# Making T4 of a two-level Strassen unit by an accumulating DMA on the GpSimd queue

## The chip, the cores and the metric

The kernel runs on one core of a Trainium2 chip. The metric is device time in microseconds (us), from the start of an execution to its end. TensorE (PE in the profile) multiplies matrices into PSUM; VectorE (DVE) and ScalarE (ACT) work on tensors in PSUM and SBUF; GpSimd (POOL) and SyncE (SP) are used here mainly to issue DMAs. Each engine works through its own queue in order and waits on semaphores for the others. A DMA that SP or GpSimd issues is carried out by 16 DMA engines that all queues share.

## The reference

The input x0 is 16384 x 1024 in bf16, there are six weight matrices ws of 1024 x 1024 and six biases bs. Each of the six layers computes

```python
x = x0
for l in range(L):                       # L = 6
    proj = jnp.einsum('bd,de->be', x, ws[l]) + bs[l]
    x = x0 * proj + x
```

## The kernel before

The rows of x0 are taken in 16 pairs of 1024 rows. A *unit* is one pair in one layer, so there are 96 units, u = 0 to 95. Inside a unit the activations lie transposed in SBUF (features on the partitions), in four quadrants B11, B12, B21, B22 of 512 features by 512 rows. `blk(xs, dh, n)` is such a quadrant, 128 partitions x 2048 bf16; B21 is `blk(xs, 1, 0)`. For the first layer of a pair they are read from the tile `x0T`, for the later ones from `xst`. There are two of each, used by alternate pairs.

The 1024 x 1024 product is done by the Strassen-Winograd scheme with seven half-size products P1 to P7 in place of eight. On the side of the activations it needs four combinations, each one VectorE instruction over 128 x 2048 (line 202):

- T1 = B12 - B11, T2 = B22 - T1, T3 = B22 - B12, T4 = B21 - T2 (lines 369 to 372).

On the side of the weights it needs the matrices W5, W6, W7, W3. They are formed once per layer, during pair 0, by `combo` (line 312), and kept in HBM in `Lc` (stored by the GpSimd queue, line 306). From pair 1 on they are loaded again for every unit, like the raw quadrants, by SP through `pump` (line 250) into a ring of 16 tiles `wp` of 512 KB. A steady unit uses nine such tiles.

The products chain in PSUM. There are four banks `pA0..3` and four banks `pX0..3`, one for each block m of 128 output features; a `group` (line 289) is four matmuls of 128 x 512 for one m. For each m:

- P1.m goes to pA[m]; P6.m, W6 times T2, is added onto it;
- F.m (ScalarE, line 294) copies pA[m] to pX[m]; P3.m, W3 times B22, is added there, and E3.m (line 298) evacuates it with the bias;
- P7.m, W7 times T3, is added onto pA[m], and E7.m evacuates it;
- P4.m, W4 times T4, is added onto pA[m], and E4.m evacuates it.

In the *steady* units, 6 to 94 (89 of them), products P5 and P2 are done by a second Strassen level, in 2 x 7 smaller groups (line 411), on quarter-size combinations of T1 and of B21 in the `ti` tiles. The units of pair 0 and the last unit (seven in all, `one` is true) do P5 and P2 in one level. After the evacuations VectorE multiplies by x0, adds x and so writes the quadrants of the next layer's x. At the end of a pair the result is turned by DMA transposes (line 538) and stored (line 544), and the x0 of a later pair is loaded by DMA transposes.

The order of the work is written out. Every operation has a rank; for steady units the table `R2` (line 26, and `EARLY[6]`, `EARLY[7]` for the first two) gives it within a unit, and a unit takes 23.4 units of rank. A heap at the end of the kernel (lines 600 to 612) issues the operation with the lowest rank among those whose predecessors have been issued. Predecessors follow from the lists of names that each operation reads and writes. The order found so is the order of every engine's queue; each engine then waits where its data is not there yet. In R2, P6 has the ranks 8.26, 9.13, 12.16 and 13.03, P3 10.86 and 13.89 to 15.62, P7 16.48 to 19.07 and P4 19.93 to 22.52. T2 has 6.93 and T4 8.4. Between the last group of P6 and the first of P4 there are three groups of P3 and the four of P7, 28 matmuls.

No operation of a steady unit uses the GpSimd queue; it stores the weight combinations of pair 0 (the last of them until about 162 us) and a part of the last unit's output.

Of the kernel before, what the change touches and what calls it, by code (L numbers as in the profile page):

```python
# [9 lines left out]
ADD = mybir.AluOpType.add  # L10
SUB = mybir.AluOpType.subtract
# [137 lines left out]
def kernel(  # L149
# [7 lines left out]
    nc = tc.nc  # L157
# [4 lines left out]
    KH = KD // 2  # L162
# [18 lines left out]
    pA = [psum.tile([P, NB], FP32, name=f"pA{i}") for i in range(KH)]  # L181
    pX = [psum.tile([P, NB], FP32, name=f"pX{i}") for i in range(KH)]
    x0Ts = [work.tile([P, 2, KD, NB], BF16, name=f"x0T{i}") for i in range(2)]
    xsts = [work.tile([P, 2, KD, NB], BF16, name=f"xst{i}") for i in range(2)]
    T = {i: work.tile([P, KH, NB], BF16, name=f"T{i}") for i in (1, 2, 3, 4)}
# [12 lines left out]
    def blk(t, dh, n):  # L198
        return t[:, n, dh * KH:(dh + 1) * KH, :]

    def tt(o, a, b, op):
        nc.vector.tensor_tensor(out=o, in0=a, in1=b, op=op)  # L202
# [50 lines left out]
    def ring_make(u, w):  # L253
        pump()
        assert ring_seq[pos["next"]] == (u, w, "make"), (u, w, ring_seq[pos["next"]])
        t = ring_tile(u, w)
        assert t is not None
        pos["next"] += 1
        return t
# [4 lines left out]
    def op(rank, fn, rd=(), wr=(), weights=()):  # L264
        for k in weights:
            uses_left[k] = uses_left.get(k, 0) + 1
        ops.append((rank, fn, tuple(rd), tuple(wr), tuple(weights)))
# [3 lines left out]
    for u, (pr, l) in enumerate(units):  # L271
        one, first, last = level1(u), u == 0, u == NU - 1
# [5 lines left out]
        XI = X0 if l == 0 else XO  # L278

        def add(name, fn, rd=(), wr=(), weights=(), rk=rk, base=base, u=u):  # L280
            op(base + rk[name], fn, rd, wr, [(u, w) for w in weights])

        def ttop(name, o, a, b, o_, rd, wr, **kw):
            add(name, lambda: tt(o, a, b, o_), rd, wr, **kw)

        def group(name, w, bank, bname, rhs, rname, m, start, u=u):
            def fn():
                for k in range(KH):
                    nc.tensor.matmul(bank[:], lhsT=wt[(u, w)][:, k, m * P:(m + 1) * P], rhs=rhs[:, k, :],  # L289
                                     start=(start and k == 0), stop=(k == KH - 1), skip_group_check=True)  # L290
            add(name, fn, rname + [f"w{u}.{w}" + ("a" if name in ("P5.0", "P5.1") and u == 0 else "")] if pr == 0 else rname, [bname], [w])

        def copy(name, dst, src, rd, wr):
            add(name, lambda: nc.scalar.copy(out=dst, in_=src), rd, wr)  # L294

        def biased(name, dst, src, eh, m, rd, wr, l=l):
            c = l * KD + eh * KH + m
            add(name, lambda: nc.scalar.activation(out=dst, in_=src, func=IDENT, bias=b_all[:, c:c + 1], scale=1.0), rd, wr)  # L298

        late = []  # L300
        if pr == 0:
            raw = lambda w, u=u: wt[(u, w)]

            def save(w, t, rd, weights=(), l=l):
                def fn():
                    nc.gpsimd.dma_start(Lc[l, CIDX[w]].rearrange("p (k e) -> p k e", k=KH), t()[:])
                if first:
                    late.append(lambda add=add: add("s" + w, fn, rd + ["gate"], (), weights))
                else:
                    add("s" + w, fn, rd, (), weights)  # L310

            def combo(w, a, b, o_, deps, u=u, raw=raw):
                def part(sl):
                    tt(raw(w)[:, :, sl], raw(a)[:, :, sl], raw(b)[:, :, sl], o_)

                def fn():
                    ring_make(u, w)
                    part(slice(0, HQ) if w == "5" and u == 0 else slice(0, H))
                rd = [f"w{u}.{d}" for d in deps]
                if w == "5" and first:  # L320
                    add("c5", fn, ["ringmake"], ["w0.5a", "ringmake"], [a, b])
                    add("c5b", lambda part=part: part(slice(HQ, H)), ["w0.5a"], ["w0.5"], [a, b])
                else:
                    add("c" + w, fn, rd + ["ringmake"], [f"w{u}.{w}", "ringmake"], [a, b])
                save(w, lambda raw=raw, w=w: raw(w), [f"w{u}.{w}"], [w])

            if first:
                gate = const.tile([P, 1], BF16, name="gate")
                late.append(lambda add=add, xst=xst, XO=XO: add("gate", lambda: nc.gpsimd.tensor_copy(gate[:], xst[:, 0, 0, 0:1]), [XO[0, 0]], ["gate"]))
            combo("5", "w12", "4", ADD, ())  # L330
            combo("6", "5", "1", SUB, ("5",))
            combo("7", "1", "w12", SUB, ())
            combo("3", "2", "6", SUB, ("6",))
            for X, s in (("2i", isum[2 * (l % 2)]), ("5i", isum[2 * (l % 2) + 1])):
                a = lambda r, c, X=X, u=u: wt[(u, X[0])][:, r * KQ:(r + 1) * KQ, c * HQ:(c + 1) * HQ]
                sv = s[:].rearrange("p q (k e) -> p q k e", k=KQ)
                rn = lambda i, X=X, l=l: f"{X}{l % 2}.{i}"
                src = [f"w{u}.5"] if X == "5i" else []

                def icombo(i, fn, rd):  # L340
                    add(X + i, fn, [rn(r) for r in rd] + src, [rn(i)], [X[0]])
                icombo("5", lambda a=a, sv=sv: tt(sv[:, 0], a(0, 1), a(1, 1), ADD), ())
                icombo("6", lambda a=a, sv=sv: tt(sv[:, 1], sv[:, 0], a(0, 0), SUB), "5")
                icombo("3", lambda a=a, sv=sv: tt(sv[:, 2], a(1, 0), sv[:, 1], SUB), "6")
                icombo("7", lambda a=a, sv=sv: tt(sv[:, 3], a(0, 0), a(0, 1), SUB), ())
                save(X, lambda s=s: s, [rn(i) for i in "5637"])

        B11, B12, B21, B22 = blk(xs, 0, 0), blk(xs, 0, 1), blk(xs, 1, 0), blk(xs, 1, 1)
        A = [f"A{m}" for m in range(KH)]
        Xn = [f"X{m}" for m in range(KH)]  # L350
        if first:

            for i, (d, n) in enumerate(TURNED):
                for k in range(KH):
                    xb = k if i < 2 else 2 + k % 2
# [11 lines left out]
                nc.vector.tensor_copy(out=b_all[:], in_=pA[KH - 1][:, 0:LK])  # L367
            add("bT", turn_bias, [], [A[KH - 1]])
        ttop("T1", T[1][:], B12, B11, SUB, [XI[0, 1], XI[0, 0]], ["T1"])
        ttop("T2", T[2][:], B22, T[1][:], SUB, [XI[1, 1], "T1"], ["T2"])  # L370
        ttop("T3", T[3][:], B22, B12, SUB, [XI[1, 1], XI[0, 1]], ["T3"])
        ttop("T4", T[4][:], B21, T[2][:], SUB, [XI[1, 0], "T2"], ["T4"])
        if not one:
            for X, Bm, src in (("5", T[1][:], "T1"), ("2", B21, XI[1, 0])):
                q = lambda dh, n, Bm=Bm: Bm[:, dh * KQ:(dh + 1) * KQ, n * NQ:(n + 1) * NQ]
# [15 lines left out]
        if not one:  # L391
            for X, Bm, src, a, b, C in (("5", T[1][:], "T1", 0, 1, P5s), ("2", B21, XI[1, 0], 2, 3, Q)):
# [5 lines left out]
                def inner(i, bank, start, X=X, u=u, q=q, t_=t_):  # L398
# [4 lines left out]
                    def fn():  # L403
# [27 lines left out]
                     ip5[X][:].unsqueeze(1).to_broadcast([P, 2, KQ, NQ]), ADD, [X + "u0", X + "u1", X + "ps"],  # L431
                     cn(0, 1) + cn(1, 1))
        for m in range(KH):
            xb = m
            group(f"P6.{m}", "6", pA[m], A[m], T[2], ["T2", A[m]], m, False)
            copy(f"F.{m}", pX[xb][:], pA[m][:], [A[m]], [Xn[xb]])
            group(f"P3.{m}", "3", pX[xb], Xn[xb], B22, [XI[1, 1], Xn[xb]], m, False)
            biased(f"E3.{m}", U[:, m, :], pX[xb][:], 0, m, [Xn[xb]], [f"U.{m}"])
            group(f"P7.{m}", "7", pA[m], A[m], T[3], ["T3", A[m]], m, False)
            biased(f"E7.{m}", V[:, m, :], pA[m][:], 1, m, [A[m]], [f"V.{m}"])  # L440
            group(f"P4.{m}", "4", pA[m], A[m], T[4], ["T4", A[m]], m, False)
            if not (last and m == KH - 1):
                biased(f"E4.{m}", W[:, m, :], pA[m][:], 1, m, [A[m]], [f"W.{m}"])
        allm = lambda s: [f"{s}.{m}" for m in range(KH)]
# [200 lines left out]
```

## Time and profile before

| | us |
|---|---|
| median of 3 runs | 2270.74 (2270.19 to 2270.76) |
| profiled execution, span | 2269.4 |
| TensorE busy | 2248.5 (99%) |
| VectorE busy | 2092.1 (92%) |
| ScalarE busy | 1847.8 (81%) |
| one 128 x 2048 subtraction on VectorE | 1.219 |
| a 512 KB weight load, issue to landing, median | 4.7 (from Lc), 5.2 (from ws) |
| a 512 KB store by the GpSimd queue, median | 6.1 (wp), 6.8 (isum) |

The profile is that of one execution, taken by the hardware profiler; its span lies 1.3 us under the median of the runs. *Busy* is the time in which an engine carries out instructions; PEld is TensorE's loading of weights, which overlaps its matmuls. The *chain* follows the work that ended last back to the start: at every step to what released it. In a row of the timeline or of a group, `out<-in` gives the tiles written and read, and xN the number of instructions. The DMA share is the mean busy share of the 16 DMA engines; since records of packets overlap it can be somewhat over 1. Times in windows are counted from the start of the span.

### The profile page before, as it was taken

What the parts mean: (1) busy time and instruction counts of PE and PEld (TensorE: products, weight loads), DVE (VectorE), ACT (ScalarE), POOL (GpSimd) and SP (SyncE); (2) the same over time, 40 slices, a digit from 0 to 9 for tenths busy, and PEclk for the clock granted to TensorE, in tenths of its full rate; (3) what the DMA queues carried; (4) which work ended last, traced back from release to release, by engine and by line L of the source; (5) the groups of instructions that cost most, each with busy time, mean ns of one, the idle gap of its engine ahead of it and who ended that gap; (6) DMA issues with size and microseconds to landing.
All of it is one profiled execution on the core that took longest, in us unless ns stands there. A gap on an engine that the chain in (4) does not pass through costs nothing.

```text
span 2269.4 us, 34750 instructions
## 1 busy us (share of the span) xinstructions
PE 2248.5 (99%) x12754; PEld 1267.4 (56%) x12993; DVE 2092.1 (92%) x2331; ACT 1847.8 (81%) x3234; POOL 24.5 (1%) x46
## 2 busy tenths in 40 slices
PE   9999999999999999999999999999999999999998
PEld 4455555555555555555555555555555555555554
DVE  8999999999999999999999999999999999999997
ACT  6678888888888888888888888888888888888887
POOL 1110000000000000000000000000000000000000
PEclk9999999999999999999999999999999999999999
DMA  8779797796977969779697796977969689696872
GB/s 279 229 270 301 251 249 264 220 303 206 251 259 224 288 220 248 264 218 288 215 266 251 227 285 205 277 242 227 288 201 294 225 225 294 195 295 224 236 247 66
DMA packets 620492, 557.02 MB, mean 245 GB/s; under 512 B 391456, under 2 KB 546592, under 8 KB 620320
## 3 DMA queue, kind: packets, MB, share of 16 engines
q1 hardware_dynamic: 614240, 534.58, 78.6%
q0 software_dynamic: 5488, 19.93, 2.3%
q8 instruction: 102, 1.67, 0.3%
q14 instruction: 70, 0.57, 0.1%
q10 hardware_dynamic: 592, 0.27, 0.0%
HBM read 437.79 MB, written 52.43 MB: 216 GB/s over the span
## 4 chain that ended last, share of the span: by engine, by line
PE 99%; issue 1%; DMA 0%; ACT 0%; SPq 0%; DVE 0%; ACTq 0%
PE pA L289 58%; PE pX L411 24%; PE pX L289 17%; DMA ev<-in_x_dram 0%; ACT pX L294 0%; PE pA L505 0%; PE pX L359 0%; PE pX L505 0%; DVE x0T L516 0%; ACT ev L294 0%; ACT x0T L363 0%; ACT ip L294 0%; SPq L577 0%; SPq L574 0%; ACTq L294 0%
## 5 line engine op out<-in xcount | busy, mean ns | idle before, releaser
L289 PEld LDWEIGHTS <-wp 128*128 128x128 bf16 x7904 | 772.9, 98 | 838.1 <-issue 0.9
L289 PE MATMUL pA<-T,wp 128*128 128x512 bf16 x4468 | 1033.0, 379 | 7.3
L298 ACT ACTIVATE ev<-pA,b_all 128x512 bf16<-128x512 f32 x1123 | 717.5, 692 | 211.2 <-PE pA L289 164.0
L411 PEld LDWEIGHTS <-wp 128*128 128x128 bf16 x4984 | 487.7, 98 | 151.5 <-issue 0.2
L202 DVE TENSOR_TENSOR ev<-ev,x0T 128x2048 bf16<-128x2048 bf16 (+2 forms) x483 | 483.0, 1002 | 8.1 <-ACT ev L298 1.5
L202 DVE TENSOR_TENSOR ev<-ev,ev 128x2048 bf16<-128x2048 bf16 (+1 forms) x283 | 343.9, 1216 | 71.7 <-ACT ev L298 44.6
L202 DVE TENSOR_TENSOR xst<-ev,xst 128x2048 bf16<-128x2048 bf16 x319 | 389.1, 1220 | 19.1 <-PE pX L289 0.9
L411 PE MATMUL pX<-ti,wp 128*128 128x256 bf16 x2848 | 397.8, 273 | 0.0
L298 ACT ACTIVATE ev<-pX,b_all 128x512 bf16<-128x512 f32 x412 | 285.4, 697 | 63.8 <-PE pX L289 62.9
L289 PE MATMUL pX<-xst,wp 128*128 128x512 bf16 x1371 | 323.3, 379 | 0.3
L289 PE MATMUL pA<-xst,wp 128*128 128x512 bf16 x1205 | 302.4, 379 | 3.9
L294 ACT CAST ev<-pX 128x512 bf16<-128x512 f32 x384 | 232.1, 606 | 47.9 <-ACT ev L298 37.4
L294 ACT COPY pX<-pA 128x512 f32<-128x512 f32 x412 | 237.5, 602 | 21.7 <-PE pA L289 18.7
L294 ACT COPY pX<-pX 128x512 f32<-128x512 f32 x356 | 207.8, 584 | 8.6 <-ACT ip L294 0.2
L202 DVE TENSOR_TENSOR T<-xst 128x2048 bf16<-128x2048 bf16 x160 | 195.0, 1218 | 0.3
L202 DVE TENSOR_TENSOR T<-xst,T 128x2048 bf16<-128x2048 bf16 x160 | 195.0, 1219 | 0.2
L294 ACT CAST iu<-pX 128x512 bf16<-128x512 f32 x356 | 192.7, 601 | 0.0
L202 DVE TENSOR_TENSOR ev<-iu,ip 128x1024 bf16<-128x1024 bf16 x178 | 123.2, 692 | 60.7 <-ACT iu L294 60.7
L411 PE MATMUL pX<-T,wp 128*128 128x256 bf16 x1068 | 160.2, 273 | 0.0
L294 ACT CAST ip<-pX 128x512 bf16<-128x512 f32 x178 | 104.7, 589 | 54.0 <-PE pX L411 54.0
L411 PE MATMUL pX<-xst,wp 128*128 128x256 bf16 x888 | 133.2, 273 | 0.1
L202 DVE TENSOR_TENSOR xst<-ev,x0T 128x2048 bf16<-128x2048 bf16 x64 | 78.3, 1223 | 1.6
(50 smaller groups left out, 636.4 us busy)
## 6 DMA issues: line engine op xcount, KB each, us to landing
wp<-Lc SPq DMA_DIRECT2D x538, 512.0 KB, 4.7
wp<-in_ws_dram SPq DMA_DIRECT2D x287, 512.0 KB, 5.2
out_dram<-x0T SPq DMA_DIRECT2D x30, 1024.0 KB, 8.8
Lc<-wp POOLq DMA_DIRECT2D x24, 512.0 KB, 6.1
Lc<-isum POOLq DMA_DIRECT2D x12, 512.0 KB, 6.8
w<-in_ws_dram SPq DMA_DIRECT2D x5, 512.0 KB, 6.1
ev<-in_x_dram SPq DMA_DIRECT2D x3, 512.0 KB, 7.2
out_dram<-x0T SPq DMA_DIRECT2D x3, 256.0 KB, 4.2
```

The lines of the kernel that those rows point to most:

```text
L202: nc.vector.tensor_tensor(out=o, in0=a, in1=b, op=op)
L289: nc.tensor.matmul(bank[:], lhsT=wt[(u, w)][:, k, m * P:(m + 1) * P], rhs=rhs[:, k, :], start=(start and k == 0), stop=(k == KH - 1), skip ...
L294: add(name, lambda: nc.scalar.copy(out=dst, in_=src), rd, wr)
L298: add(name, lambda: nc.scalar.activation(out=dst, in_=src, func=IDENT, bias=b_all[:, c:c + 1], scale=1.0), rd, wr)
L411: nc.tensor.matmul(pX[bank][:, m * NQ:(m + 1) * NQ], lhsT=wv[:, k, m * P:(m + 1) * P], rhs=rhs[:, k, :], start=(start and m == 0 and k == ...
```

## The change

In the steady units T4 is no longer a VectorE instruction with a tile of its own. T2 is formed with the other sign, T1 - B22. A DMA on the GpSimd queue then adds B21 onto T2 in place, element by element, so that the tile holds B21 + T1 - B22 = T4, and P4 reads that tile. Since P6 reads the same tile with its earlier content, the DMA comes after all four groups of P6; to that end the loop that adds P6 and F is split from the one that adds P3, P7 and P4. W6 is formed with the other sign, so that P6 stays the same, and W3's formula, which contains W6, is turned to match. T4's rank stays the same, but its name now reads and writes "T2". The seven units with one level make T4 on VectorE as before, with the sign turned.

```diff
-            combo("6", "5", "1", SUB, ("5",))
+            combo("6", "1", "5", SUB, ("5",))
             combo("7", "1", "w12", SUB, ())
-            combo("3", "2", "6", SUB, ("6",))
+            combo("3", "2", "6", ADD, ("6",))
...
-        ttop("T2", T[2][:], B22, T[1][:], SUB, [XI[1, 1], "T1"], ["T2"])
+        ttop("T2", T[2][:], T[1][:], B22, SUB, [XI[1, 1], "T1"], ["T2"])
         ttop("T3", T[3][:], B22, B12, SUB, [XI[1, 1], XI[0, 1]], ["T3"])
-        ttop("T4", T[4][:], B21, T[2][:], SUB, [XI[1, 0], "T2"], ["T4"])
+        if one:
+            ttop("T4", T[4][:], B21, T[2][:], ADD, [XI[1, 0], "T2"], ["T4"])
+        else:
+            pass
+        T4 = (T[4], "T4") if one else (T[2], "T2")
...
         for m in range(KH):
+            group(f"P6.{m}", "6", pA[m], A[m], T[2], ["T2", A[m]], m, False)
+            copy(f"F.{m}", pX[m][:], pA[m][:], [A[m]], [Xn[m]])
+        if not one:
+            add("T4", lambda B21=B21: nc.gpsimd.dma_start(T[2][:], B21, accum_op=ADD), [XI[1, 0], "T2"], ["T2"])
+        for m in range(KH):
             xb = m
-            group(f"P6.{m}", "6", pA[m], A[m], T[2], ["T2", A[m]], m, False)
-            copy(f"F.{m}", pX[xb][:], pA[m][:], [A[m]], [Xn[xb]])
             group(f"P3.{m}", "3", pX[xb], Xn[xb], B22, [XI[1, 1], Xn[xb]], m, False)
             biased(f"E3.{m}", U[:, m, :], pX[xb][:], 0, m, [Xn[xb]], [f"U.{m}"])
             group(f"P7.{m}", "7", pA[m], A[m], T[3], ["T3", A[m]], m, False)
             biased(f"E7.{m}", V[:, m, :], pA[m][:], 1, m, [A[m]], [f"V.{m}"])
-            group(f"P4.{m}", "4", pA[m], A[m], T[4], ["T4", A[m]], m, False)
+            group(f"P4.{m}", "4", pA[m], A[m], T4[0], [T4[1], A[m]], m, False)
```

## The prediction

> **What bounds the kernel now.** I read the page's busy times first, then the chain that ended last, the groups that touch the T tiles, the timeline around one steady unit's P6 to P4, and last how busy the DMA engines are in that stretch. From the page (busy time, two DMA queues, the chain by engine, two groups):
>
> ```profile
> PE 2248.5 (99%) x12754; PEld 1267.4 (56%) x12993; DVE 2092.1 (92%) x2331; ACT 1847.8 (81%) x3234; POOL 24.5 (1%) x46
> q1 hardware_dynamic: 614240, 534.58, 78.6%
> q0 software_dynamic: 5488, 19.93, 2.3%
> PE 99%; issue 1%; DMA 0%; ACT 0%; SPq 0%; DVE 0%; ACTq 0%
> L289 PE MATMUL pA<-T,wp 128*128 128x512 bf16 x4468 | 1033.0, 379 | 7.3
> L202 DVE TENSOR_TENSOR T<-xst,T 128x2048 bf16<-128x2048 bf16 x160 | 195.0, 1219 | 0.2
> ```
>
> TensorE is the chain: 99% of it, and 2269.4 - 2248.5 = 20.9 us of idle time in the whole span. Matmuls that read a T tile were preceded by 7.3 us of idle time in all. So whatever VectorE gains can give back next to nothing, and a new wait of TensorE is paid in full. The page also prices the GpSimd queue's DMA: q0 moved 38 x 512 KB, and its packets took 2.3% of sixteen engines for 2269.4 us, so 52.2 / 38 = 1.37 us of all engines for 512 KB.
>
> The timeline of a steady unit (layer 3; start, duration, engine, line, operation, operands, count):
>
> ```profile
> 798.56 1.89 PE L289 MATMUL pA<-T,wp 128*128 128x512 bf16 x7
> 800.28 2.75 PE L289 MATMUL pX<-xst,wp 128*128 128x512 bf16 x12
> 802.87 5.99 PE L289 MATMUL pA<-T,wp 128*128 128x512 bf16 x27
> ```
>
> The first row is P6.2 and P6.3 (8 matmuls, a record is missing), the second is P3 for three banks, the third begins with 16 matmuls of P7 and goes on with P4. Twelve matmuls take 802.87 - 800.28 = 2.59 us, 0.216 each. The last P6 matmul starts at about 800.06 and ends 0.379 later, at 800.44; P4 starts 16 x 0.216 after 802.87, at 806.33. That leaves **5.9 us** between the end of P6 and P4. It is the only cover the new DMA has.
>
> Busy time by stretch, for the same stretch of six consecutive units, layers 0 to 5 (length, busy by engine, then clock, DMA share, GB/s):
>
> ```profile
> 729.70:736.00 6.30, 6.25 (x30) 2.87 (x30) 5.70 (x5) 4.63 (x9) 0.00 (x0) 1.00 0.96 270
> 753.10:759.40 6.30, 6.30 (x31) 2.85 (x30) 5.70 (x5) 4.64 (x9) 0.00 (x0) 1.00 1.14 223
> 776.50:782.70 6.20, 6.15 (x29) 2.81 (x29) 5.60 (x5) 4.53 (x9) 0.00 (x0) 1.00 1.07 376
> 799.90:806.10 6.20, 6.20 (x30) 2.78 (x29) 5.60 (x5) 4.54 (x9) 0.00 (x0) 1.00 0.85 280
> 823.20:829.50 6.30, 6.25 (x30) 2.85 (x30) 5.70 (x5) 4.63 (x9) 0.00 (x0) 1.00 0.84 277
> 846.60:852.90 6.30, 6.30 (x31) 2.87 (x30) 5.70 (x5) 4.63 (x9) 0.00 (x0) 1.00 0.86 271
> ```
>
> The DMA share is 0.84 to 1.14: just there the engines are occupied by weight loads, and in layers 0 to 2 by the turning of x and the stores as well.
>
> **The change, part by part.** Sums are made against the profiled execution (span 2269.4); the median of the runs, 2270.7, lies 1.3 above it, which I carry over.
>
> *Signs.* W6, W3 and T2 get the other sign by swapped operands: same instructions, cost 0. The seven units of one level (layers of pair 0 and the last unit) keep T4 on VectorE: 0.
>
> *Removed.* 89 subtractions on VectorE (T4 of units 6 to 94), 89 x 1.219 = 108 us, 1.2 us a unit. TensorE does not wait for them, so between 0 and -7.3 us (all idle time ahead of matmuls from T); I take 0.
>
> *T2's buffer is held longer*, until P4 has read it instead of P6. The next T2 is issued behind other VectorE work: around 1270 to 1296 P4 ended at 1277.6 and T2 started at 1284.5, 6.9 us later. That cover moves with TensorE, so 0.
>
> *Added: one DMA a unit on the GpSimd queue.* It waits for P6.3's last matmul, because it overwrites what P6 reads. Nothing else stands in that queue in these units, so nothing is queued behind its wait. P4's first weight load waits for its landing, and TensorE works in order: everything of P4 and of the next unit stands behind it. Hand-overs: a ScalarE evacuation in the same stretch starts 0.17 us after its matmuls; with one such step at each end, 5.9 - 0.3 = **5.6 us** remain from issue to landing.
>
> How long from issue to landing? No accumulating DMA is in the trace. The nearest rows are the plain 512 KB stores of this queue in pair 0, one in a lull and one in a full stretch (0.79 and 1.04 DMA share while in flight), and a weight load of 512 KB by SP inside this stretch, in layers 3 and 2:
>
> ```profile
> L306 POOL DMA_DIRECT2D Lc<-wp x1: 534/534/534, 115.1 to 115.1; - x1
> DMA to landing us min/median/max: 3.0/3.0/3.0
> ...
> L306 POOL DMA_DIRECT2D Lc<-isum x1: 534/534/534, 161.9 to 161.9; - x1
> DMA to landing us min/median/max: 7.3/7.3/7.3
> ...
> L250 SPq DMA_DIRECT2D wp<-in_ws_dram x1: 383/383/383, 800.5 to 800.5; - x1
> DMA to landing us min/median/max: 4.8/4.8/4.8
> ...
> L250 SPq DMA_DIRECT2D wp<-in_ws_dram x1: 383/383/383, 777.1 to 777.1; - x1
> DMA to landing us min/median/max: 7.9/7.9/7.9
> ```
>
> So 3.0 us is the floor, of which 1.37 is moving. Accumulating reads two streams and writes one; bounds for the moving are 1.37 us (the second read is free) and 5.5 (four passes of a plain one). I take two passes, 2.75, since a stream that must be read is the nearest thing to a stream that is moved: alone 4.4 us. Beside other traffic:
> - Layers 3 to 5: SP's load took 4.8 against 3.2 for its fastest ones (the same load issued 13 us earlier), 1.6 us of waiting for one pass. For two passes 1.6 to 3.2: 6.0 to 7.6. I take 6.6, stall 1.0.
> - Layers 1 and 2: the store in the full stretch waited 7.3 - 3.0 = 4.3 us for one pass, so 8.7 to 13. I take 9.0, near the low end, since some of that store's wait was for its own queue's earlier stores: stall 3.4.
> - Layer 0: full at both ends with a lull of about 1.5 us between. I take 7.5: stall 1.9.
>
> The rest of the unit follows TensorE, so a stall lengthens the unit one for one. Layers 0 to 4 come 15 times, layer 5 fourteen times: 15 x (1.9 + 3.4 + 3.4 + 1.0 + 1.0) + 14 x 1.0 = 174.5 us.
>
> *More DMA work for the weights.* 2.75 us per 23.4 us unit is a share of 0.12 on top of 0.83 (mean over units from 1223.6 to 1364.0). Where it is over 1 (layers 1 and 2) loads fall back by a few us, but the ring holds 16 tiles and a unit uses 9, so a load is asked for most of a unit ahead; and the stalls give time back. I take 0; the upper bound is one stall of 2.75 in the two full units, 30 x 2.75 = 82 us.
>
> Sum: 2270.7 + 174.5 = **2445 us**.
>
> [...] In that lull the store at 115.1 was issued in 534 ns and landed in 3.0 us while VectorE was busy 3.00 of 3.00 us with additions and subtractions of tensors. [...]
>
> The granted clock is 1.00 in every row above, and TensorE has no long pause in these units. [...]
>
> **Rivals.**
> 1. *It lands in time, no change:* the point is 5.6 us from issue to landing. For it: single stores of this queue issued at 115.1, 118.5 and 110.4 took 3.0, 5.2 and 5.3 us in stretches of DMA share 0.79, 0.90 and 0.76, about as in layers 3 to 5. Against it: layers 1 and 2, and the second read. In time everywhere: 2268 to 2273. In time in layers 3 to 5 and 0, late by 1 to 2 us in layers 1 and 2: 2300 to 2330.
> 2. *The addition is slow,* four passes (5.5 us): alone 3.0 + 4.1 = 7.1 us, beside the traffic 9 to 13, stalls of 3.4 to 7.4, so 2570 to 2930. For it: the destination must be read before it is written, row by row. Against it: only that nothing in the trace shows it.
> 3. *VectorE's relief counts:* at best the 7.3 us above, 2263, and only if rival 1 holds as well.
>
> **How the numbers follow.** A measurement can tell a change of 0.2%, 4.5 us, from none. Forecast, stalls of 0.8 to 3.4 us in the mean, 2340 to 2570: 0.48. Rival 1: 0.07 for no change, 0.15 for the partly late one. Rival 2: 0.28. Rival 3: 0.02. The low end takes in the partly late case; the high end takes in most of the slow addition: 2295 to 2770. Faster 0.02, same 0.07, slower 0.91.
>
> **What would show it.** DVE has 89 fewer instructions in T<-xst,T and T<-x0T,T; POOL issues 89 DMAs into T; the chain names a DMA into T; the idle time before matmuls pA<-T rises from 7.3 to about 175 us, waits of one kind, longest in layers 1 and 2; the landing is 6 to 9 us. I am wrong if the landing's median is under 5.6 (rival 1) or over 9.5 (rival 2), or if a clock under 1.00 or waits for wp loads make up a good part of the loss.

## The result, and the profile after

The changed kernel takes 2579.2 us (median of 4 runs, 2554.9 to 2595.8), the one before 2270.8 us. By the medians 308 us are lost. The ratio of the fast runs is 1.132, with an interval of 1.129 to 1.136, or 300 us; it leaves out the run of 2595.8 us, which counts as slow. The profiled execution is the fastest of the four (span 2553.1 us), so the profile accounts for 2553.1 - 2269.4 = 283.7 us. The other three runs had granted clocks of 0.962 to 0.969; what else they lost on top is in no trace.

From the page after: busy time, the two DMA queues, and the groups that answer to those shown of before.

```profile
PE 2326.1 (91%) x12754; PEld 1276.9 (50%) x12993; DVE 1999.9 (78%) x2242; ACT 1851.0 (72%) x3234; POOL 100.7 (4%) x135
q1 hardware_dynamic: 614240, 534.58, 69.6%
q0 software_dynamic: 18304, 66.59, 11.6%
L289 PE MATMUL pA<-T,wp 128*128 128x512 bf16 x4468 | 1111.5, 396 | 213.1 <-DMA T<-xst 180.8
L202 DVE TENSOR_TENSOR T<-T,xst 128x2048 bf16<-128x2048 bf16 x80 | 97.3, 1216 | 0.2
```

VectorE has 2331 - 2242 = 89 instructions less and 92 us less work, and TensorE's share fell from 99% to 91%. The idle time ahead of matmuls on T tiles rose from 7.3 to 213.1 us, and its releaser is the DMA into T. The second number of that row matters too: a matmul of this group now takes 396 ns in the mean in place of 379, though nothing about the matmuls was changed. The 89 DMAs take 11.6% x 2553.1 - 52.2 (the plain ones, as before) = 244 us of all engines, 2.74 us each: two passes. The chain of waits breaks off after 2% of this span, so I read the waits themselves. TensorE's waits, longest first (engine, line, waited for: us in total, times, longest):

```profile
PE pA L289 <- DMA T<-xst: 180.8, 73, 4.1
PE pA L289 <- DMA T<-x0T: 23.0, 12, 4.3
```

The DMAs themselves, and the core's mean granted clock:

```profile
L441 POOL DMA_DIRECT2D T<-xst x74: 847/856/874, 198.9 to 2511.1; - x74
L441 POOL DMA_DIRECT2D T<-x0T x15: 849/856/879, 169.8 to 2403.0; - x15
DMA to landing us min/median/max: 4.9/8.1/9.7
...
core 0: 2553.1 us, clock 0.971
```

So 85 of 89 DMAs were waited for, 203.8 us in all, and the landing has a median of 8.1 us against the 5.6 that the cover allows. The rest is in the clock: a mean of 0.971 means that 0.029 x 2553.1 = 74 us of full-speed time were lost (an upper bound for its cost, since TensorE stood still in a part of that time). Together 278 of the 283.7 us. The timeline of TensorE in two units shows how the two hang together (P7 first, then P4):

```profile
865.06 3.62 PE L289 MATMUL pA<-T,wp 128*128 128x512 bf16 x15
871.32 5.17 PE L289 MATMUL pA<-T,wp 128*128 128x512 bf16 x16 [2.64 <-DMA T<-xst]
...
919.19 3.62 PE L289 MATMUL pA<-T,wp 128*128 128x512 bf16 x15
924.51 3.61 PE L289 MATMUL pA<-T,wp 128*128 128x512 bf16 x16 [1.71 <-DMA T<-xst]
```

After a wait of 1.71 us the 16 matmuls of P4 take 3.61 us, as always. After one of 2.64 us they take 5.17. The stretches behind that wait (length, busy by engine, then granted clock, DMA share, GB/s) tell why:

```profile
872.00:873.00 1.00, 1.00 (x4) 0.32 (x3) 0.00 (x0) 0.00 (x0) 0.00 (x0) 0.50 0.48 195
875.00:876.00 1.00, 1.00 (x6) 0.49 (x5) 0.00 (x0) 1.00 (x3) 0.00 (x0) 1.00 0.00 0
```

The clock was halved, and came back some 3.4 us later. This happened in 40 stretches of the execution, 148 us in all; 39 of them stand behind a wait for the DMA, 38 of these of more than 2 us, and one is the end of the execution. The trace also shows which waits it takes. In its clock records all 40 stretches begin at whole multiples of 3.413 us from one another, so in this trace what counts is a window on a fixed grid. Here are the windows of that grid that hold the two waits, the longer one first, with the window that follows it (same columns):

```profile
867.66:871.07 3.41, 1.02 (x5) 0.28 (x3) 3.38 (x4) 1.75 (x4) 0.00 (x0) 1.00 1.01 281
871.08:874.49 3.41, 3.17 (x8) 1.17 (x9) 0.92 (x1) 0.00 (x0) 0.00 (x0) 0.50 0.43 174
922.28:925.69 3.41, 1.70 (x9) 0.65 (x8) 3.38 (x4) 1.27 (x3) 0.00 (x0) 1.00 0.99 332
```

In the first TensorE was busy for 1.02 of 3.41 us, and half clock followed; in the last for 1.70, and it did not. The same holds for the whole execution from 30 us on: in the 39 windows at full clock that half clock followed, TensorE was busy for at most 42%; in the 657 others for at least 41%. So a wait of 2 us was enough where it fell into one window, and a longer one that was split between two windows was not: the shortest wait that half clock followed took 1.98 us, the longest that it did not follow 3.34.

### The profile page after: what moved, and what is told of

Its sections match the earlier page's. It is cut to its first block, busy times and chain, and to the rows that moved or that the text cites. A ratio compares the mean times of both kernels' runs of the same rounds, so it can differ in the third digit from the quotient of the medians.

```text
span 2553.1 us, 34912 instructions
## 1 busy us (share of the span) xinstructions
PE 2326.1 (91%) x12754; PEld 1276.9 (50%) x12993; DVE 1999.9 (78%) x2242; ACT 1851.0 (72%) x3234; POOL 100.7 (4%) x135
## 3 DMA queue, kind: packets, MB, share of 16 engines
q0 software_dynamic: 18304, 66.59, 11.6%
## 5 line engine op out<-in xcount | busy, mean ns | idle before, releaser
L289 PE MATMUL pA<-T,wp 128*128 128x512 bf16 x4468 | 1111.5, 396 | 213.1 <-DMA T<-xst 180.8
L441 POOL DMA_DIRECT2D T<-xst x74 | 63.3, 856 | 1905.8 <-PE pA L289 1850.9
L202 DVE TENSOR_TENSOR T<-T,xst 128x2048 bf16<-128x2048 bf16 x80 | 97.3, 1216 | 0.2
```

The lines of the kernel that those rows point to most:

```text
L441: add("T4", lambda B21=B21: nc.gpsimd.dma_start(T[2][:], B21, accum_op=ADD), [XI[1, 0], "T2"], ["T2"])
```

## The experiments

My theory after the result had three parts: P4 waits for the landing; the landing is long because the addition reads twice and because weight loads use the same DMA engines; and the wait is paid a second time through the clock. The rivals: the clock dip is harmless; the additional DMA work makes weights late; the landing is a fixed property of this queue; the shared tile costs, whoever writes it.

**1. Keeping TensorE busy in the wait.**

```diff
+        if rk is R2:                                   # rank 19.5, between P7 and P4
+            def fill():
+                for _ in range(10):
+                    nc.tensor.matmul(pX[3][:], lhsT=zeros[:, 0:P], rhs=zeros[:], start=True, stop=True, ...)
+            add("Z", fill, [], [Xn[3]])
```

> Ten matmuls on zeros, 2.2 us, stand between P7 and P4 in units 8 to 94, so that TensorE is never idle for long while the DMA lands. Theory A (waiting costs twice: the idle time, and the half clock that follows it): the granted clock goes from 0.971 to above 0.99, a unit is lengthened by the longer of 2.2 us and the old stall (mean 2.85 us worked out from the stalls of the changed kernel), 2505 to 2540 us. Theory B (the clock dip costs nothing of its own, all 308 us are the wait): as the changed kernel or above it, 2575 to 2610 us.

Measured: 2524.8 us, ratio 1.111 (1.109 to 1.114). The core, the waits for the DMA and the landing:

```profile
core 0: 2524.1 us, clock 0.999
...
PE pA L289 <- DMA T<-xst: 50.3, 58, 3.3
PE pA L289 <- DMA T<-x0T: 6.2, 3, 4.2
...
DMA to landing us min/median/max: 4.9/8.3/9.7
```

The landing is as late as before, each unit has 2.2 us more matmuls to do, and yet the kernel is 54 us faster by the medians, 48 by the ratios. The half clock is a real part of the loss. The two profiled executions give its size: the filler adds 87 x 2.16 = 188 us of matmuls, the waits for the DMA fell from 203.8 to 56.5 us, by 147, and the span fell by 2553.1 - 2524.1 = 29. That leaves 188 - 147 + 29 = 70 us for the clock, just under the 74 that the profile gives as its upper bound.

**2. A plain copy in place of the addition.**

```diff
-            add("T4", lambda B21=B21: nc.gpsimd.dma_start(T[2][:], B21, accum_op=ADD), ...)
+            add("T4", lambda B21=B21: nc.gpsimd.dma_start(T[2][:], B21), ...)
```

> The DMA copies B21 over T2 and adds nothing, so T4 is left out of the computation; waits, queue, place and bytes sent stay. Theory A (the second read makes the landing long, a 4 KB packet goes from 0.328 to 0.16 us): landing 5 to 6.5 us, stalls under 1 us, 2275 to 2350 us. Theory B (the landing is mostly queueing behind weight loads and the fixed part of this queue): landing over 7 us, 2450 us or more.

Measured: 2386.4 us, 1.051 (1.048 to 1.054); between the two expectations. The DMAs:

```profile
L441 POOL DMA_DIRECT2D T<-xst x74: 528/531/540, 195.3 to 2351.0; - x74
...
DMA to landing us min/median/max: 2.8/6.6/16.6
```

P4 now multiplies B21 in place of T4. One pass less takes 1.5 us off the landing and 193 us off the time (by the medians), most of the loss, since it also leaves only 8 waits of over 2 us, and the mean clock at 0.992. But a plain copy would be late as well: 6.6 us is above the cover, where I had expected 5 to 6.5.

**3. The DMA beside an unchanged T4.**

```diff
+        ttop("T4", T[4][:], B21, T[2][:], ADD, [XI[1, 0], "T2"], ["T4"])
...
+        op(base + 13.1, lambda: nc.gpsimd.dma_start(isum[3][:], P5s[:], accum_op=ADD), [...], ["S"])
```

> T4 is made by VectorE in its own tile as before; in each steady unit the GpSimd queue still sends an accumulating DMA of 512 KB, after 5cc, from P5's tile onto a tile that nobody reads later. Theory A (the loss is the wait of P4 and what follows from it): 2268 to 2280 us, PE 99% busy. Theory B (the additional DMA work delays weight loads or the turning of x, or GpSimd's descriptors disturb VectorE): 2300 us or more, with waits for wp or longer VectorE instructions.

Measured: 2275.8 us, 1.0024 (1.0015 to 1.0033). Busy time, the DMA, and the waits for weights:

```profile
PE 2247.9 (99%) x12754; PEld 1267.2 (56%) x12993; DVE 2091.7 (92%) x2331; ACT 1847.9 (81%) x3234; POOL 100.8 (4%) x135
...
isum<-ev POOLq DMA_DIRECT2D x89, 512.0 KB, 8.4
...
PEld L289 <- DMA wp<-Lc: 3.3, 1, 3.3
PE pA L289 <- DMA wp<-Lc: 2.8, 1, 2.8
```

The same 89 DMAs, landing just as late (8.4 us) but waited for by nobody, cost about 5 us. VectorE's busy time is 2091.7 us against 2092.1 before, so its instructions are not longer. So the loss is P4's wait and what follows from it; what the traffic does to others is about these 5 us.

**4. A longer cover: P6.2 and P6.3 earlier.**

```diff
-2p6@7.39 5p4@7.82 P6.0@8.26 P6.1@9.13 2p7@9.99 2p3@10.43 P3.0@10.86 2p4@11.73 P6.2@12.16 P6.3@13.03 P3.1@13.89
+2p6@7.39 5p4@7.82 P6.0@8.26 P6.1@9.13 P6.2@9.14 P6.3@9.15 2p7@9.99 2p3@10.43 P3.0@10.86 2p4@11.73 P3.1@13.89
```

> In R2 the groups P6.2 and P6.3 follow P6.1 at once, ahead of 2p7, 2p3, P3.0 and 2p4: the cover between the end of P6 and P4 grows from 5.9 to about 8.1 us. Theory A (the cover decides): stalls fall from a mean of 2.7 to 0.3 to 1.2 us, too short for a half clock, 2290 to 2390 us. Theory B (the landing is set by traffic that ends at a fixed point of the unit, so that an earlier issue lands no earlier): 2500 us or more. If ScalarE now holds up P3, waits for pX show in place of it.

Measured: 2470.5 us, 1.090 (1.087 to 1.093): faster by 109 us, but far from the expected 2290 to 2390. TensorE's waits and the landing:

```profile
PE pX L289 <- ACT pX L294: 70.9, 88, 0.8
PE pA L289 <- DMA T<-xst: 48.4, 13, 18.0
PE pA L289 <- DMA T<-x0T: 11.0, 3, 4.8
...
DMA to landing us min/median/max: 4.5/8.2/26.9
```

The cover works: only 16 DMAs are waited for in place of 85, at an unchanged median landing. But my edit brought two other things. P3 now waits 0.8 us in every unit for ScalarE's copy F into pX, because the 2p groups that free these banks come later. And some landings became very long; the longest, 26.9 us, lies in a stretch in which x0 is turned by DMA transposes.

**5. T4 in place by VectorE.**

```diff
-            add("T4", lambda B21=B21: nc.gpsimd.dma_start(T[2][:], B21, accum_op=ADD), ...)
+            add("T4", lambda B21=B21: tt(T[2][:], B21, T[2][:], ADD), ...)
```

> T4 is still formed in T2's tile after P6, but by one VectorE addition in place of the DMA. Theory A (the order and the shared tile cost nothing, the DMA's landing does): 2267 to 2276 us. Theory B (a tile that P6 must first give up makes P4 late whoever writes it): 2300 us or more, with waits of P4 for VectorE.

Measured: 2390.9 us, 1.053 (1.051 to 1.055). Theory A fell, and B's waits are not there either:

```profile
DVE T L202 <- PE pA L289: 130.1, 89, 1.6
...
PE pX L415 <- DVE ti L202: 77.0, 88, 0.9
```

The expected 2267 to 2276 us of theory A are missed by 115. P4 does not wait at all. VectorE waits 1.5 us a unit for P6 to give up the tile, and all that stands behind it in its queue is late, down to the `ti` tiles that the next unit's products need. This is the wait that the GpSimd queue, with nothing behind it, avoids. Run 12 takes it apart.

**6. Half of T4 by DMA.**

```diff
+            def halves(B21=B21):
+                tt(T[2][:, 0:KQ], B21[:, 0:KQ], T[2][:, 0:KQ], ADD)
+                nc.gpsimd.dma_start(T[2][:, KQ:KH], B21[:, KQ:KH], accum_op=ADD)
```

> The DMA adds only the second half of T4 (256 KB); VectorE adds the first half in place. Theory A (landing grows with the bytes that are read, so that two passes of 256 KB equal one pass of 512 KB): as the plain copy, landing 6 to 6.8 us, 2330 to 2400 us. Theory B (the fixed part and the queueing of this queue make up nearly all): landing over 7 us, 2450 us or more. Theory C (well under the cover): landing under 5.6 us, 2270 to 2300 us.

Measured: 2355.8 us, 1.038 (1.036 to 1.041), the landing has a median of 6.6 us. Two passes of 256 KB land as late as one pass of 512 KB (6.6), as theory A has it: by these two runs the bytes that are read decide that part.

**7. The early P6, and the DMA in layers 2 to 5 only** (`dv = one or l < 2` chooses VectorE).

> P6.2 and P6.3 early as in the run before, and the DMA only in layers 2 to 5; layers 0 and 1, in which x is turned by transposes, make T4 on VectorE in its own tile. Theory A (cover in layers 2 to 5, the long landings beside transposes in layers 0 and 1, and a wait of P3 for ScalarE's copy that the early P6 brings, about 0.8 us a unit, make up the 200 us of that run): 0.8 x 87 + 0.4 x 59 = 93 us above before, 2345 to 2385 us, clock above 0.998. Theory B (the early order costs more elsewhere): 2420 us or more.

Measured: 2371.4 us, 1.044 (1.042 to 1.046), clock 0.999, in the range of theory A. TensorE's waits:

```profile
PE pX L289 <- ACT pX L294: 70.8, 88, 0.8
PE pA L289 <- DMA T<-xst: 3.2, 6, 1.1
```

With 8.1 us of cover and no transposes, the DMA is waited for 3.2 us in all, in 59 units, at a median landing of 8.2 us. What remains is largely the wait for ScalarE that my order of P6 causes.

**8. No weight loads.**

```diff
+            if units[u][0] >= 2:
+                wt[(u, w)] = wt[(2 * L - 1, "4")]
+                pos["next"] += 1
+                continue
```

> From pair 2 on no weights are loaded: all units use one tile that was loaded in pair 1, so the products are other ones than the reference's; everything else stays, the turning and storing of x too. Theory A (weight loads on the same 16 DMA engines make the accumulating DMA late): in layers 2 to 5 landing 4.6 to 5.4 us and no stall, stalls only in layers 0 and 1, 2272 to 2330 us. Theory B (the accumulating DMA takes 7 us or more by itself): 2450 us or more.

Measured: 2347.2 us, 1.034 (1.030 to 1.038), above the expected range. TensorE's waits and the landing over all units, and the landing of five successive units, from layer 4 of a pair to layer 2 of the next:

```profile
PE pA L293 <- DMA T<-x0T: 42.9, 15, 4.0
PE pA L293 <- DMA T<-xst: 10.9, 7, 3.3
...
DMA to landing us min/median/max: 4.5/4.6/9.6
...
L445 POOL DMA_DIRECT2D T<-xst x4: 856/856/856, 714.0 to 810.6; - x4
L445 POOL DMA_DIRECT2D T<-x0T x1: 856/856/856, 760.8 to 760.8; - x1
DMA to landing us min/median/max: 4.5/4.5/8.4
```

Alone, the accumulating DMA lands in 4.5 us, well within the cover. The one at 8.4 us is the one of layer 0, issued at 760.8. What runs beside it is the storing of the finished pair rather than the turning of x, as the SP queue and the landings of these 8.4 us show:

```profile
760.18 4.93 SPq L555 DMA_DIRECT2D out_dram<-x0T  x2
769.56 11.95 SPq L544 DMA_TRANSPOSE x0T<-in_x_dram  x2
...
out_dram<-x0T SPq DMA_DIRECT2D x2, 1024.0 KB, 11.6
T<-x0T POOLq DMA_DIRECT2D x1, 512.0 KB, 8.4
```

The two stores of 1 MB were issued within 1.3 us and the first is in flight through its whole landing; the transpose before them, issued at 754.6, landed after 6.9 us, and those of the next x0 are issued at 769.6, after it. These layers make up most of the loss: of the 53.8 us that TensorE's matmuls waited, 42.9 were for DMAs of layer 0 (out of x0T). That they alone would cost so much I had not expected. So about 3.5 us of the usual 8.1 come from weight loads.

**9. A quarter by DMA, three quarters by VectorE in their own tile at the old place.**

```diff
+            ttop("T4", T[4][:, 0:3], B21[:, 0:3], T[2][:, 0:3], ADD, [XI[1, 0], "T2"], ["T4"])
...
+            add("T4", lambda B21=B21: nc.gpsimd.dma_start(T[2][:, 3:KH], B21[:, 3:KH], accum_op=ADD), ...)
...
+            rhs4 = T[4] if one else [T[4] if k < 3 else T[2] for k in range(KH)]
```

> VectorE makes three quarters of T4 in a tile of their own at the old place; the DMA adds only the last quarter (128 KB) onto T2 after P6, and only the fourth matmul of a P4 group reads it, so the cover is 5.9 + 0.65 - 0.45 = 6.1 us. Theory A (landing = a fixed part, the passes and the wait beside the loads; from 8.1 us for 512 KB and 6.6 for 256 KB about 5.8 for 128 KB): stalls of 0 to 0.4 us, 2270 to 2300 us, and not below 2268, since no work of VectorE that is saved is on the path. Theory B (what this queue waits for beside the loads has nothing to do with the size): landing over 6.5 us, 2310 us or more.

Measured: 2301.5 us, 1.014 (1.012 to 1.015). The landing's median is 5.7 us, as worked out, and TensorE waited 26.8 us for 28 of the 89 DMAs; the time is 1 us over the range. The loss grows with the size: 31 us for 128 KB, 308 for 512 KB. Even 128 KB is not free, and nothing of VectorE's relief shows.

**10. Half by DMA, VectorE's half in its own tile** (as in 9, with 2 in place of 3).

> As the run with half of T4 by DMA (2356 us), but VectorE's half goes to a tile of its own at the old place, so VectorE does not wait for P6. Cover 5.9 + 0.43 - 0.45 = 5.9 us. Theory A (in the earlier run a part of the loss was VectorE held back behind its wait for P6, the rest the landing of 6.6 us): stalls of about 0.7 us alone, 2310 to 2345 us, and no waits of matmuls for ti tiles. Theory B (VectorE's wait cost nothing there): 2350 us or more.

Measured: 2372.0 us, 1.042 (1.037 to 1.047), with runs from 2350 to 2377; not better than run 6, so theory A fell: VectorE's half-size wait had not been the cause there, and run 6 shows no wait of TensorE for `ti` tiles. The landing's median is again 6.6 us, but three DMAs of layer 1 took 11.5 us and more, where run 6 had none over 8.7.

**11. The same, with layer 1 left to VectorE** (`n4 = KH if l == 1 else 2`).

> As the run with half of T4 by DMA and VectorE's half in a tile of its own (2372 us), but in layer 1, in which the next x0 is being turned by DMA transposes, all of T4 is made by VectorE. Theory A (that run's excess over the one in which VectorE held the DMA back, 2356 us, comes from long landings beside the turns in layer 1, up to 11.9 us): no landing over 9 us, 2305 to 2335 us. Theory B (the excess has another cause): 2340 us or more.

Measured: 2335.4 us, 1.029 (1.027 to 1.030), at the upper edge of theory A's range; landing 3.3/6.5/9.0. Leaving out 15 of 89 DMAs takes away 37 of 102 us, so layer 1 had more than its share, with the landings beside the transposes of x0. Why these met in run 10 and not in run 6 was not tested; in both the DMA starts 0.30 us after the last matmul of P6.

**12. T4 by VectorE, late, but in its own tile.**

```diff
+            add("T4", lambda B21=B21: tt(T[4][:], B21, T[2][:], ADD), [XI[1, 0], "T2"], ["T2", "T4"])
```

> T4 by VectorE as in the in-place run (2391 us) and at the same place in VectorE's queue, but into its own tile, so that it does not wait for P6. Theory A (the 120 us of that run are VectorE held behind its wait for P6, 1.5 us a unit, which makes the ti tiles late for the next unit): 2267 to 2280 us and no waits for ti. Theory B (the late place in VectorE's queue costs it, not the wait): 2350 us or more.

Measured: 2280.3 us, 1.004 (1.003 to 1.006), at the upper edge of theory A's range, and TensorE's wait for `ti` is down from 77.0 to 0.2 us. At the same place of the queue, without the wait for P6, 111 of run 5's 120 us are gone. The wait in VectorE's queue was the cause there. The remaining 9.5 us are in no wait that the trace shows; TensorE's busy time is 2255.9 - 2248.5 = 7.4 us longer.

No version beats the kernel before. None could by much: TensorE was busy for 99% of it.

## Why the prediction was right, and where it was off

*The mechanism* of the loss was right: P4 waits for the landing (run 3: without the waiting 5 us of loss), the cover is about 5.6 us, VectorE's relief is worth nothing, the weight loads do not come late (run 3), and the stall lengthens the unit. The time lies in the range, but 134 us above the 2445 us of the sum, and also above 2340 to 2570, the stretch that the forecast had for itself. What held it was the room above 2570 that was left for rival 2, whose mechanism the runs exclude. That part is luck. By the medians, 29 us of the 134 are waits for the DMA (203.8 against 174.5), about 70 the clock, and the rest is not traced: 25 us by which the median run is slower than the profiled one, and some 10.

*Own work of the DMA:* taken as two passes, 2.75 us, and 4.4 us from issue to landing when alone. Measured: 2.74 and 4.5 (run 8). Rival 2, four passes, is excluded.

*Waiting beside other traffic* was mis-sized for layers 3 to 5. I had taken 2.2 us over the lone landing, scaled from SP's own weight loads, which waited 1.6. A row had been misread for it: the load of 3.2 us issued 13 us earlier is one from Lc, not the same load from ws, of which none in the trace before landed in under 3.5 us. The medians by layer, read from the trace, are 7.3, 8.3, 8.5, 8.3, 7.5 and 8.1 us for layers 0 to 5, against 7.5, 9.0, 9.0 and three times 6.6. So the wait is 3.0 to 3.8 us there. Nor does it scale with the passes, as I had supposed: the plain copy of run 2 waits 6.6 - 3.0 = 3.6 us, the addition 8.1 - 4.5 = 3.6. The mean landing of 7.87 us less 5.6 of cover, 89 times, is 202 us; the waits listed are 203.8. I had 174.5: too much in layers 1 and 2, too little in layers 3 to 5.

*The granted clock* was the larger miss. The sum priced it at nothing, for stalls of 1.0 to 3.4 us; that stalls of this length leave the clock alone was not shown by the rows of before, all at a clock of 1.00. In the changed kernel half clock followed 39 of the 85 waits, the shortest of them 1.98 us, and run 1 shows that it costs, some 70 us. One of the signs of being wrong that I had named, a clock under 1.00 as a good part of the loss, has thus come true. Nor was TensorE idle for the whole of each window of 3.413 us that half clock followed: 58% was enough in one of them.

*VectorE beside the DMA* rightly has no term in the sum: in run 8 the DMA landed in 4.5 us beside a VectorE that was busy for 85% of the span, and in run 3 the 89 DMAs left VectorE's busy time at 2091.7 us, against 2092.1 before.

*Rival 1* had its point right: in run 8, landings under 5.6 us cost nothing, and so does the longer cover in run 7.

## What to carry to other kernels

Work that is moved from a busy engine to a DMA must land inside the time between its last input and its first reader; count that time in matmuls first, and compare it with the landing beside the traffic of that very stretch, not with a lone one. Saved work on an engine that nobody waits for buys nothing (92 us of VectorE's here). A wait on TensorE can cost more than its length: matmuls that do nothing useful were worth some 50 us here. And an in-place update puts a wait for the old content's readers into the writer's queue (1.5 us a unit in run 5), with everything that stands behind it.

## What the runs showed of the hardware that was not expected

The clock: in the changed kernel waits of TensorE of about 2 to 3 us were followed by 3.4 us at half clock. Of its 85 waits for the DMA, one of the 24 under 2 us was followed by it, 13 of the 19 from 2 to 2.5 us, and 25 of the 42 longer ones. What tells them apart in this trace is not the length but how busy TensorE was in a window of the 3.413 us grid: at most 42% where half clock followed, at least 41% elsewhere (above). Run 4 has a longer case: from 1866 to 1874 us TensorE was busy for 0.00 us, at a clock of 0.50 throughout.

In run 4 a DMA of the GpSimd queue between two tiles in SBUF and two DMA transposes, in flight in the same stretch, all took far longer than elsewhere. DMA issues from 1850 to 1878 us, with KB and us to landing, and the queues in that stretch:

```profile
DMA packets 5253, 2.31 MB, mean 82 GB/s; under 512 B 4997, under 2 KB 4997, under 8 KB 5253
...
T<-xst POOLq DMA_DIRECT2D x1, 512.0 KB, 26.9
x0T<-in_x_dram SPq DMA_TRANSPOSE x2, 19.1
```

Here 512 KB took 26.9 us in place of this run's median of 8.2, and the two transposes 19.1 in the median in place of the 7.3 of before, at 82 GB/s with a DMA share of 1.19 to 1.34 from 1854 us on, and TensorE stood still for 18 us. In run 2 the longest landing of a plain copy took 16.6 us, against a median of 6.6. Only 16 of run 4's 89 DMAs were waited for at all; what start times bring the long landings about was not tested.
